# A fused cross-attention and snake MLP on one core: slot tables per block, six batches transposed by DMA, and the squares split between two engines

## The chip, the cores and the metric

One Trainium2 chip, one of its cores. The metric is the device time of one execution, in microseconds (us), and where several runs are shown, their median. Engines: PE (TensorE, matmuls), DVE (VectorE), ACT (ScalarE), POOL (GpSimd) and SP (SyncE, which here only issues DMAs). Each engine takes its instructions strictly in the order of the program; an instruction that waits holds up all behind it on its engine.

## The reference

Eight batches of eight heads; each head has 512 tokens `x` and 32 state rows `state`, both of width 64. Tokens attend to state rows and state rows to tokens; the results, 544 rows per batch, go through an MLP with a snake activation.

```python
scores  = scale * x @ state.T;  a  = softmax(scores);   xread = a @ state     # 512 rows
scores2 = scale * state @ x.T;  a2 = softmax(scores2);  sread = a2 @ x        # 32 rows
y = concat([xread, sread])                     # per head; heads side by side: 4352 x 512
h = y @ w_in                                   # 512 -> 2048
g = h + sin(alpha * h)**2 / (alpha + 1e-9)     # snake
out = g @ w_out                                # 2048 -> 512
```

## The kernel before

The work is a sequence of nine blocks `t`. Blocks 0 to 7 are the 512 token rows of one batch each; block 8 holds the 256 state rows of all batches. A block has 16 slots, one for each 128 columns `f` of the hidden width. Slot `f` of block `t` runs, in the order of the code:

- `mm1(t, f)`: two matmuls into one of four PSUM buffers `h_ps`, then ACT's sine into `s`, then the square `s2 = s * s` on POOL. The token side never forms `xread`: `m_step` multiplies the state rows into `w_in` beforehand (the tile `M`, four steps per batch, cast from PSUM by ACT and DVE), and `mm1` multiplies `M` by the transposed softmax weights `AT`.
- the PE steps that the dictionary `pe` holds for this slot: pieces of the attention of batch `n = t + 1`, and `m_step`.
- `snake`, with a lag of two slots: DVE forms `h + s2 / alpha` from `s2` and `h_ps` into `gT`, which frees the `h_ps` buffer. So `mm1` of slot `f + 4` waits for `snake` of slot `f`.
- the second matmuls `mm2` of the block before (four per slot from block 2 on); when 16 are done ACT copies the sum to `o_sb`, and SP stores it.
- the steps that the dictionary `post` holds.

The attention of a batch consists of `pack` (DVE copies the loaded tile `xnat` to `xp`), `T` (eight PE transposes for each half `g`, and a DVE copy from PSUM to `xT`), `S` (scores), `X` (ACT's exponential `E`, which needs another function table than the sine), `Rs` (row sums and reciprocals on DVE), `N` (normalised weights `A`, on POOL), `AT_` (eight PE transposes and one DVE copy to `AT`), `W` and `Cs` (the state side, with a reciprocal `rC` on DVE). All score, transpose, state and `M` tiles share two PSUM buffers (`tag="px"`).

The order is written out by hand, in `plan(t)`: a tuple of slots for each kind of step, one set for block 0 and one for all others. For block 1 on it reads:

```python
ts, ss, xs, rs, ats = (0, 1), (3, 4), 4, 7, 12
ms = ((9, True, False), (11, True, False), (13, True, False), (15, True, False))
ps = (13, 14)
```

`ts` are the slots of `T`, `ss` of `S`, `xs` of both `X`, `ats` of `AT_`, `ms` of `m_step` with who casts each half (True is ACT), `ps` of `pack` for batch `t + 2`, whose load was issued in slot 5.

Of the kernel before, what the change touches and what calls it, by code (L numbers as in the profile page):

```python
# [10 lines left out]
ALU = mybir.AluOpType  # L11
AX = mybir.AxisListType
BF16 = mybir.dt.bfloat16
FP32 = mybir.dt.float32
U32 = mybir.dt.uint32


@with_exitstack
def kernel(
# [16 lines left out]
    G = 2  # L36
# [13 lines left out]
    apool = ctx.enter_context(tc.tile_pool(name="apool", bufs=2))  # L50
    epool = ctx.enter_context(tc.tile_pool(name="epool", bufs=3))
    smallp = ctx.enter_context(tc.tile_pool(name="smallp", bufs=2))
# [58 lines left out]
    xs_all = const.tile([P, Q, B * Ns], BF16, name="xs_all")  # L111

    def warm_up(n):
        wp = psH.tile([P, S], FP32, name="h_ps")
        for _ in range(n):
            nc.tensor.matmul(wp[:], warm[:, 0:P], warm[:], start=True, stop=True)


    def prep_state():
# [23 lines left out]
    class Att:  # L143
# [2 lines left out]
            a.xp = xppool.tile([P, C, H, D], BF16, name="xp")  # L146

        def alloc(a):
            a.xT = apool.tile([P, Q, S], BF16, name="xT")
# [17 lines left out]
        def T(a, g):  # L167
            tp = psX.tile([P, 2, S], BF16, name="x_ps", tag="px")
            for k in range(2):
                for i in range(C):  # L170
                    nc.tensor.transpose(  # L171
                        tp[:, k, i * P:(i + 1) * P], a.pair(i, 2 * g + k), ident[:]
                    )
            nc.vector.tensor_copy(a.xT[:, 2 * g:2 * g + 2, :], tp[:])  # L174

        def S(a, g):
            sp = psX.tile([P, C, P], FP32, name="s_ps", tag="px")
            for i in range(C):
                for k in range(2):
                    cols = slice(k * 2 * Ns, (k + 1) * 2 * Ns)  # L180
                    nc.tensor.matmul(  # L181
                        sp[:, i, cols],
                        a.xT[:, 2 * g + k, i * P:(i + 1) * P],
                        stT[:, a.b * G + g, cols],
                        start=True, stop=True,
                    )
            a.sp[g] = sp
# [185 lines left out]
    a.AT_([1])  # L373

    def plan(t):
        pe, post = {}, {}

        def add(d, s, fn, *args):  # L380
            d.setdefault(s, []).append((fn, args))

        def nxt(b, k):
            if k == 0:
                atts[b] = Att(b)
            atts[b].pack(k)

        def att(b, m, *args):
            getattr(atts[b], m)(*args)

        n = t + 1
        if t == 0:
            for k in range(2):
                add(post, 0, nxt, 1, k)
            add(pe, 5, m_step, 0, 2, (True, False))
            add(pe, 7, m_step, 0, 3, (True, False))
            ts, ss, xs, rs, ats = (1, 2), (3, 4), 4, 8, 13
            ms, ws = ((9, True, True), (11, True, False), (14, True, False), (15, True, False)), []
            ps = (15, 15)
        else:  # L400
            ts, ss, xs, rs, ats = (0, 1), (3, 4), 4, 7, 12
            ms = ((9, True, False), (11, True, False), (13, True, False), (15, True, False))
            ws = [(6, 7, t)] if n < B else [(0, 1, t)][:B - t]
            if t == 1:
                ws.append((10, 10, 0))
            ps = (13, 14)
        if n < B:
            add(pe, ts[0], att, n, "alloc")
            for g in range(G):
                add(pe, ts[g], att, n, "T", g)  # L410
                add(pe, ss[g], att, n, "S", g)
                add(post, xs, att, n, "X", g)
                add(post, rs + g, att, n, "Rs", g)
                add(post, rs + 1 + g, att, n, "N", g, nc.gpsimd)
            add(pe, ats, att, n, "AT_", [0, 1])
            for k, (s, *on) in enumerate(ms):
                add(pe, s, m_step, n, k, on)
        for s0, s1, b in ws:
            add(pe, s0, att, b, "W")
            add(pe, s1, att, b, "Cs")  # L420
        if t + 2 < B:
            add(post, 5, load_x, t + 2, 1)
            for k in range(2):
                add(post, ps[k], nxt, t + 2, k)

        two = {}
        if t == 0:
            for f in range(9, FT):  # L430
                two[f] = [(0, st, 2 * (f - 9), 2 * (f - 8)) for st in range(2)]
        elif t == 1:
            two[1] = [(0, 0, 14, 16), (0, 1, 14, 16)]
            for f in range(2, FT):
                k0, k1 = 32 * (f - 2) // 14, 32 * (f - 1) // 14
                for h in range(2):
                    a0, a1 = max(k0, 16 * h), min(k1, 16 * h + 16)
                    if a0 < a1:
                        two.setdefault(f, []).append((0, 2 + h, a0 - 16 * h, a1 - 16 * h))
# [55 lines left out]
```

## Time and profile before

| | |
|---|---|
| median of 3 runs | 261.21 us (260.61 to 261.88) |
| the profiled execution, its own time | 260.04 us |
| its span, first to last instruction | 258.3 us |
| mean granted clock of PE | 0.973 |
| busy: PE, DVE, ACT, POOL | 231.3, 169.7, 158.9, 171.4 us |
| blocks 3, 4 and 5, from first `mm1` to first `mm1` | 26.32 us each |

The profiled execution's own time is 1.74 us over its span and 1.17 us under the median. A block's length is read from the time at which the first `mm1` of each block starts: 15.26 (block 0), 43.72, 69.58, 95.90, 122.22, 148.54, 174.86, 201.05 (block 7) and 223.06 us (block 8); the last matmul ends at 251.0 us.

### The profile page before, as it was taken

Reading aid. Unit: us, or ns where it says so; the run is one execution under the profiler, and the core shown is the slowest. Engines: PE = TensorE matmul, PEld = TensorE weight load, DVE = VectorE, ACT = ScalarE, POOL = GpSimd, SP = SyncE. Lnnn points to the kernel's source line nnn. Section 1 sums busy time; section 2 is a strip of 40 time slices with the busy share of each in tenths; the row PEclk is TensorE's granted clock in tenths of the full one; section 3 lists DMA queues with packets and bytes.
Section 4 is the critical chain, followed back from the end, with each engine's and each line's share of the span. In section 5 each row is a group of like instructions: output and inputs, shape, how many; then the busy total and the mean of one; then the engine's idle time right before and its main releaser. Section 6 shows DMA issues by size and latency. Waiting matters only on the chain.

```text
span 258.3 us, 4499 instructions
## 1 busy us (share of the span) xinstructions
PE 231.3 (90%) x1676; PEld 110.7 (43%) x1676; DVE 169.7 (66%) x279; ACT 158.9 (62%) x251; POOL 171.4 (66%) x183
## 2 busy tenths in 40 slices
PE   7575798778999999989998999899999999999980
PEld 2442143333454345434543454345534444555560
DVE  3654857669984897498849884988497765533300
ACT  2668854694759565956595659565966566544410
POOL 8744884649864986498649864996397678744400
PEclk9979599999999999999999999999999999999997
DMA  7999930208011811181118111711111111211111
GB/s 82 195 205 205 203 49 4 82 1 124 0 43 41 122 43 41 41 123 43 43 41 120 46 42 41 121 44 41 44 41 43 41 41 41 83 41 41 44 54 68
DMA packets 19793, 17.85 MB, mean 69 GB/s; under 512 B 2876, under 2 KB 15420, under 8 KB 19772
## 3 DMA queue, kind: packets, MB, share of 16 engines
q0 software_dynamic: 12704, 8.65, 23.6%
q1 hardware_dynamic: 6936, 8.79, 10.2%
q8 instruction: 13, 0.21, 0.3%
q10 hardware_dynamic: 132, 0.13, 0.1%
q14 instruction: 8, 0.07, 0.1%
HBM read 17.31 MB, written 8.91 MB: 102 GB/s over the span
## 4 chain that ended last, share of the span: by engine, by line
PE 69%; DVE 19%; DMA 4%; issue 2%; POOL 2%; ACT 2%; ACTq 0%; POOLq 0%
PE o_ps L314 36%; PE h_ps L288 18%; DVE gT L305 7%; DMA xnat<-in_x_dram 4%; PE m_ps L269 3%; DVE rC L244 3%; PE h_ps L294 3%; DVE R L194 3%; PE x_ps L171 3%; DVE M L280 2%; DVE xs_all L247 2%; PE w_ps L226 1%; PE o_ps L339 1%; PE a_ps L217 1%; DVE rR L195 1%
## 5 line engine op out<-in xcount | busy, mean ns | idle before, releaser
L301 POOL TENSOR_TENSOR s<-s 128x512 bf16<-128x512 bf16 (+1 forms) x144 | 141.5, 992 | 70.5 <-ACT s L299 70.3
L314 PE MATMUL o_ps<-w_out_sb,gT 128*128 128x512 bf16 x528 | 137.3, 382 | 2.6 <-DVE gT L305 2.6
L299 ACT ACTIVATE s<-h_ps,alpha_sb 128x512 bf16<-128x512 f32 (+1 forms) x144 | 94.3, 664 | 72.3 <-PE h_ps L288 61.1
L305 DVE SCALAR_TENSOR_TENSOR gT<-s,inva_sb,h_ps 128x512 bf16<-128x512 bf16 (+1 forms) x144 | 100.1, 711 | 32.0 <-POOL s L301 31.7
L288 PE MATMUL h_ps<-AT,M 128*128 128x512 bf16 x256 | 78.5, 389 | 7.6 <-DVE gT L305 7.1
L314 PEld LDWEIGHTS <-gT 128*128 128x128 bf16 x528 | 46.7, 98 | 52.5 <-issue 6.9
L288 PEld LDWEIGHTS <-M 128*128 128x128 bf16 x256 | 24.9, 99 | 40.5 <-issue 14.3
L280 DVE CAST M<-m_ps 128x512 bf16<-128x512 f32 x29 | 19.6, 676 | 11.5 <-PE m_ps L269 11.4
L320 ACT COPY o_sb<-o_ps 128x512 f32<-128x512 f32 x33 | 19.3, 588 | 9.2 <-PE o_ps L314 7.8
L278 ACT CAST M<-m_ps 128x512 bf16<-128x512 f32 x31 | 17.8, 578 | 0.6 <-PE m_ps L269 0.6
L244 DVE RECIPROCAL rC<-w_ps 128x128 f32<-128x128 f32 x8 | 7.7, 957 | 15.3 <-PE w_ps L237 15.3
L269 PE MATMUL m_ps<-w_in_sb,stT 64*32 64x512 bf16 x240 | 13.5, 401 | 2.8 <-ACT E L190 2.1
L174 DVE COPY xT<-x_ps 128x1024 bf16<-128x1024 bf16 x16 | 11.0, 690 | 5.1 <-PE x_ps L171 4.7
L269 PEld LDWEIGHTS <-stT 64*32 64x32 bf16 x256 | 3.9, 90 | 19.3 <-issue 17.9
L159 DVE COPY xp<-xnat 128x1024 bf16<-128x1024 bf16 x16 | 10.2, 649 | 2.6 <-DMA xnat<-in_x_dram 2.5
L171 PE MATMUL x_ps<-ident,xp 128*128 128x128 bf16 x128 | 10.3, 226 | 1.5 <-ACT stT L140 1.4
L171 PEld LDWEIGHTS <-xp 128*128 128x128 bf16 x128 | 8.9, 102 | 6.0 <-issue 1.7
L194 DVE TENSOR_REDUCE R<-E 128x16 f32<-128x512 bf16 x16 | 10.9, 680 | 0.2 <-ACT E L190 0.2
L190 ACT ACTIVATE E<-s_ps 128x512 bf16<-128x512 f32 x16 | 8.8, 595 | 1.4 <-PE s_ps L181 1.3
L294 PE MATMUL h_ps<-xs_all,w_in_sb 128*128 128x256 bf16 x64 | 9.6, 273 | 0.0
L190 ACT ACT_TABLE_LOAD x7 | 9.0, 1283 | 0.1
L299 ACT ACT_TABLE_LOAD x7 | 9.0, 1283 | 0.1
(46 smaller groups left out, 116.5 us busy)
## 6 DMA issues: line engine op xcount, KB each, us to landing
out_dram<-o_sb SPq DMA_DIRECT2D x33, 256.0 KB, 2.2
xnat<-in_x_dram POOLq DMA_DIRECT2D x7, 512.0 KB, 7.7
w_in_sb<-in_moe_w_in_dram POOLq DMA_DIRECT2D x4, 512.0 KB, 11.0
w_out_sb<-in_moe_w_out_dram POOLq DMA_DIRECT2D x4, 512.0 KB, 19.3
xnat<-in_x_dram POOLq DMA_DIRECT2D x2, 256.0 KB, 5.6
st_nat<-in_state_dram POOLq DMA_DIRECT2D x1, 256.0 KB, 4.5
out_dram<-o_sb SPq DMA_DIRECT2D x1, 128.0 KB
out_dram<-o_sb ACTq DMA_DIRECT2D x1, 128.0 KB
```

Of the source, the lines that this page charges most:

```text
L171: nc.tensor.transpose(tp[:, k, i * P:(i + 1) * P], a.pair(i, 2 * g + k), ident[:])
L190: nc.scalar.activation(a.E[:, g], a.sp[g][:], ACT.Exp, scale=scale)
L194: nc.vector.reduce_sum(a.R[:, g], E8, axis=AX.X)
L269: nc.tensor.matmul(mp[g][o0:o0 + Ns, :], stT[rows, b * G + g, c0:c0 + Ns], w_in_sb[rows, 2 * g + h, fs * FW:(fs + 1) * FW], start=True, st ...
L278: nc.scalar.copy(dst, mp[g][:])
L280: nc.vector.tensor_copy(dst, mp[g][:])
L288: nc.tensor.matmul(hp[:, :n], Ms[t][:, g, f * P:(f + 1) * P], atts[t].AT[:, g, :], start=(g == 0), stop=(g == G - 1),)
L299: nc.scalar.activation(s[:, :n], hp[:, :n], ACT.Sin, scale=alpha_sb[:, f:f + 1])
L301: nc.gpsimd.tensor_tensor(s2[:, :n], s[:, :n], s[:, :n], ALU.mult)
L305: nc.vector.scalar_tensor_tensor(gT[t][:, f, :n], s2[:, :n], inva_sb[:, f:f + 1], hp[:, :n], ALU.mult, ALU.add)
L314: nc.tensor.matmul(op[:], gT[t][:, ft, st * P:(st + 1) * P], w_out_sb[:, ft, :], start=(ft == 0), stop=(ft == FT - 1),)
L320: nc.scalar.copy(o_sb[:], op[:])
```

## The change

- **Tables.** `plan(t)` takes its slots from a table `PLAN` with one entry each for blocks 0, 1, 2 to 6, 7 and 8. The two `X` of a batch may stand in different slots (1 and 5 in blocks 2 to 6), the two `N` may run on different engines (`Nd` lists the halves that DVE takes), and the casts of `M` are given step by step (`MA`). The number of `mm2` per slot is a table too (`two`, `TWO0`, `TWO1`).
- **Transposes by DMA.** For batches 2 to 7 one DMA issued by SP, `T_dma`, transposes the whole `xp` into `xT` (512 KB), a block ahead of its use; another, `AT_dma`, transposes `A` into `AT` (256 KB). The PE transposes and the DVE copies of these batches are gone. Batches 0 and 1 keep them.
- **Squares.** The squares of the slots in `sq` are made by DVE, one slot later and behind that slot's `snake`; 58 of the 144, 35 of them in blocks 2 to 6 (seven each).
- **Buffers.** `xT`, `A`, `AT`, `M` and the small tiles have three buffers in place of two.
- **Ends.** Five more warm-up matmuls stand between the first two `m_step` of block 0; the last store is issued by SP and not by ACT.

```diff
+ 2: {'S': (1, 3), 'X': (1, 5), 'R': (2, 5), 'N': (5, 5), 'A': 5, 'W': (1, 1),
...
+        def T_dma(a):
+            nc.sync.dma_start_transpose(
+                a.xT[:].rearrange("p i q t -> p (i q) t"),
+                a.xp[:].rearrange("p i h d -> p (i h d)"),
+            )
+
+        def AT_dma(a):
+            nc.sync.dma_start_transpose(
+                a.AT[:].rearrange("p g (i t) -> p (g i) t", i=C),
+                a.A[:].rearrange("p g i c -> p (g i c)"),
+            )
...
-        nc.gpsimd.tensor_tensor(s2[:, :n], s[:, :n], s[:, :n], ALU.mult)
+        if f in PLAN[kind(t)]["sq"]:
+            late.append((s2, s, n))
+        else:
+            nc.gpsimd.tensor_tensor(s2[:, :n], s[:, :n], s[:, :n], ALU.mult)
...
+    def squares():
+        while late:
+            s2, s, n = late.pop(0)
+            nc.vector.tensor_tensor(s2[:, :n], s[:, :n], s[:, :n], ALU.mult)
...
-    warm_up(12)
+    warm_up(WARM[0])
...
-    for k in range(2):
-        m_step(0, k, (True, True))
+    m_step(0, 0, (True, True))
+    warm_up(WARM[1])
+    m_step(0, 1, (True, True))
...
+            if t == 0:
+                add(pe, p["A"], att, n, "AT_", [0, 1])
+            else:
+                add(post, p["A"], att, n, "AT_dma")
...
+            add(post, p["L"], load_x, t + 2, 1)
+            add(post, p["P2"][0], first, t + 2)
             for k in range(2):
-                add(post, ps[k], nxt, t + 2, k)
+                add(post, p["P2"][k], att, t + 2, "pack", k)
+            add(post, p["T2"], att, t + 2, "T_dma")
```

In blocks 2 to 6 the table puts `S` in slots 1 and 3, `W` and `Cs` in slot 1, `m_step` in 7, 9, 12 and 14, `pack` in 8 and 10, `T_dma` in 11 and `AT_dma` in 5. In block 0 `T_dma` stands in slot 13 (`pack` in 12), and `S` of that batch in slot 0 of block 1. In block 1 `AT_dma` stands in slot 13, and its `AT` is read by the first `mm1` of block 2.

SP's whole queue, before: one small load, and then the stores.

```order
L68 DMA alpha_sb<-in_moe_alpha_dram 128x16x1
L326 DMA out_dram<-o_sb 128x512 x32
L330 DMA out_dram<-o_sb 4x32x512
L330 DMA out_dram<-o_sb 4x32x256
L490 UNCONDITIONAL_BRANCH
```

SP's queue of the changed kernel, from its start to the stores of block 4.

```order
L122 DMA alpha_sb<-in_moe_alpha_dram 128x16x1
L238 DMA_TRANSPOSE xT<-xp 128x16x128
L408 DMA out_dram<-o_sb 128x512 x3
L238 DMA_TRANSPOSE xT<-xp 128x16x128
L244 DMA_TRANSPOSE AT<-A 128x8x128
L408 DMA out_dram<-o_sb 128x512 x2
L244 DMA_TRANSPOSE AT<-A 128x8x128
L408 DMA out_dram<-o_sb 128x512 x2
L238 DMA_TRANSPOSE xT<-xp 128x16x128
L408 DMA out_dram<-o_sb 128x512 x2
L244 DMA_TRANSPOSE AT<-A 128x8x128
```

Blocks 2 to 5 each have two transposes among their four stores; each transpose waits on SP for the engine that made its input (DVE's `pack`, POOL's `N`).

ACT in the first half of a block in the middle, before: both exponentials of a batch (`E`) stand together between two table loads.

```order
L299 ACTIVATE s<-h_ps,alpha_sb 128x512
L190 ACT_TABLE_LOAD
L190 ACTIVATE E<-s_ps 128x512 x2
L299 ACT_TABLE_LOAD
L299 ACTIVATE s<-h_ps,alpha_sb 128x512 x3
L320 COPY o_sb<-o_ps 128x512
```

The same place in block 3 of the changed kernel.

```order
L263 ACT_TABLE_LOAD
L263 ACTIVATE E<-s_ps 128x512
L372 ACT_TABLE_LOAD
L372 ACTIVATE s<-h_ps,alpha_sb 128x512 x2
L402 COPY o_sb<-o_ps 128x512
L372 ACTIVATE s<-h_ps,alpha_sb 128x512 x2
L263 ACT_TABLE_LOAD
L263 ACTIVATE E<-s_ps 128x512
L372 ACT_TABLE_LOAD
L372 ACTIVATE s<-h_ps,alpha_sb 128x512
L402 COPY o_sb<-o_ps 128x512
```

The exponentials are apart, with two table loads each: four loads in a block where there were two (24 against 14 over all blocks).

DVE at the end of one block and the beginning of the next, before.

```order
L159 COPY xp<-xnat 128x4x256
L280 CAST M<-m_ps 128x512
L305 SCALAR_TENSOR_TENSOR gT<-s_1209,inva_sb,h_ps 128x512
L174 COPY xT<-x_ps 128x1024
L305 SCALAR_TENSOR_TENSOR gT<-s_1235,inva_sb,h_ps 128x512
L174 COPY xT<-x_ps 128x1024
L305 SCALAR_TENSOR_TENSOR gT<-s_1248,inva_sb,h_ps 128x512
```

DVE in the last slots of block 3 and the first of block 4 of the changed kernel; `s_...<-s` is a square.

```order
L217 COPY xp<-xnat 128x4x256
L387 SCALAR_TENSOR_TENSOR gT<-s_1438,inva_sb,h_ps 128x512
L353 CAST M<-m_ps 128x512
L387 SCALAR_TENSOR_TENSOR gT<-s_1459,inva_sb,h_ps 128x512
L384 TENSOR_TENSOR s_1476<-s 128x512
L384 TENSOR_TENSOR s_1487<-s 128x512
L387 SCALAR_TENSOR_TENSOR gT<-s_1476,inva_sb,h_ps 128x512
L387 SCALAR_TENSOR_TENSOR gT<-s_1487,inva_sb,h_ps 128x512
L387 SCALAR_TENSOR_TENSOR gT<-s_1510,inva_sb,h_ps 128x512
L384 TENSOR_TENSOR s_1521<-s 128x512
L384 TENSOR_TENSOR s_1543<-s 128x512
L387 SCALAR_TENSOR_TENSOR gT<-s_1521,inva_sb,h_ps 128x512
```

The two copies of `xT` are gone, and squares stand in pairs ahead of the snakes that read them.

## Rows read from the trace of the kernel before

**Rows 1.** The page's first part: busy us, share of the span and instructions of each engine.

```profile
PE 231.3 (90%) x1676; PEld 110.7 (43%) x1676; DVE 169.7 (66%) x279; ACT 158.9 (62%) x251; POOL 171.4 (66%) x183
```

**Rows 2.** Busy time of each engine in blocks 0, 1 and 3.

```profile
core 0: us, PE busy (x) PEld busy (x) DVE busy (x) ACT busy (x) POOL busy (x), PEclk, DMA share, GB/s
15.26:43.72 28.46, 22.76 (x149) 8.94 (x149) 18.11 (x31) 18.27 (x28) 19.54 (x19) 0.82 0.84 134
43.72:69.58 25.86, 21.65 (x189) 10.07 (x188) 19.72 (x34) 17.44 (x27) 18.16 (x19) 1.00 0.28 52
...
95.90:122.22 26.32, 25.64 (x193) 11.96 (x192) 20.22 (x33) 18.18 (x29) 19.21 (x20) 1.00 0.29 61
```

**Rows 3.** Waits inside block 3: who waited for whom, us, times, longest.

```profile
ACT s L299 <- PE h_ps L288: 7.6, 9, 1.2
...
PE h_ps L288 <- DVE gT L305: 0.7, 2, 0.5
```

**Rows 4.** PE's timeline around block 3: start, us, instruction; the first `mm1` of six slots.

```profile
89.38 0.59 PE L288 MATMUL h_ps<-AT,M 128*128 128x512 bf16 x2
...
91.12 0.59 PE L288 MATMUL h_ps<-AT,M 128*128 128x512 bf16 x2
...
92.86 0.60 PE L288 MATMUL h_ps<-AT,M 128*128 128x512 bf16 x2
...
97.64 0.60 PE L288 MATMUL h_ps<-AT,M 128*128 128x512 bf16 x2
...
99.38 0.60 PE L288 MATMUL h_ps<-AT,M 128*128 128x512 bf16 x2
...
100.68 0.60 PE L288 MATMUL h_ps<-AT,M 128*128 128x512 bf16 x2
```

**Rows 5.** Groups in block 3: busy us, mean ns of one.

```profile
L280 DVE CAST M<-m_ps 128x512 bf16<-128x512 f32 x5 | 3.4, 673 | 0.8 <-PE m_ps L269 0.8
L278 ACT CAST M<-m_ps 128x512 bf16<-128x512 f32 x5 | 2.9, 577 | 0.0
...
L174 DVE COPY xT<-x_ps 128x1024 bf16<-128x1024 bf16 x2 | 1.4, 692 | 0.5 <-PE x_ps L171 0.4
...
L190 ACT ACT_TABLE_LOAD x1 | 1.3, 1283 | 0.0
...
L220 DVE COPY AT<-a_ps 128x1024 bf16<-128x1024 bf16 x1 | 0.7, 691 | 0.4 <-PE a_ps L217 0.4
```

**Rows 6.** Timeline of POOL and DVE, at 12 us and at 94 us.

```profile
12.49 1.06 POOL L202 TENSOR_TENSOR A<-E,rR 128x512 bf16<-128x512 bf16 x1
...
13.26 0.85 DVE L205 TENSOR_TENSOR A<-E,rR 128x512 bf16<-128x512 bf16 x1
...
94.32 1.04 POOL L301 TENSOR_TENSOR s<-s 128x512 bf16<-128x512 bf16 x1 [0.62 <-ACT s L299]
...
94.57 1.07 DVE L159 COPY xp<-xnat 128x1024 bf16<-128x1024 bf16 x1
```

**Rows 7.** All copies of `xp`: shortest, median and longest ns.

```profile
L159 DVE COPY xp<-xnat x16: 411/572/1073, 7.1 to 173.5; 128x1024 bf16<-128x1024 bf16 x16
```

**Rows 8.** The page's DMA parts: SP's queue (packets, MB, share), and issues to landing.

```profile
q1 hardware_dynamic: 6936, 8.79, 10.2%
...
out_dram<-o_sb SPq DMA_DIRECT2D x33, 256.0 KB, 2.2
xnat<-in_x_dram POOLq DMA_DIRECT2D x7, 512.0 KB, 7.7
```

**Rows 9.** Bytes moved in 40 slices of 100 to 112 us, a lone store in it.

```profile
GB/s 0 0 0 0 0 0 0 0 0 0 0 0 48 396 369 62 0 0 0 0 0 0 0 0 0 0 0 0 0 0 0 0 0 0 20 341 239 205 118 123
```

**Rows 10.** Bytes moved in 40 slices of the first 50 us.

```profile
GB/s 0 3 41 177 182 152 191 203 206 209 197 199 202 205 207 212 201 208 207 206 204 207 207 206 199 194 186 29 0 0 0 13 0 0 7 0 0 7 0 200
```

**Rows 11.** DVE's longest wait in blocks 0 and 1 (15.26 to 69.58 us).

```profile
DVE M L280 <- PE m_ps L269: 6.5, 5, 3.0
```

More of the change, by code (lines that the diff above doesn't have):

```diff
@@ L15 @@
 U32 = mybir.dt.uint32
+PLAN = {0: {'P': (0, 0),
+     'T': (1, 1),
+     'S': (2, 2),
+     'X': (3, 3),
+     'R': (3, 8),
+     'N': (9, 10),
+     'A': 15,
+     'M0': (5, 8),
+     'M': (9, 11, 12, 14),
+     'MA': ((1, 0), (1, 1), (1, 1), (1, 1)),
+     'L': 1,
+     'P2': (12, 12),
+     'T2': 13,
+     'sq': (0, 9, 10, 12, 13),
+     'Nd': ()},
+ 1: {'S': (0, 2),
+     'X': (2, 2),
+     'R': (4, 7),
+     'N': (4, 7),
+     'A': 13,
+     'W': (4, 5),
+     'W0': (10, 11),
+     'M': (7, 8, 12, 14),
+     'MA': ((1, 0), (1, 1), (1, 1), (1, 1)),
+     'L': 2,
+     'P2': (9, 10),
+     'T2': 10,
+     'sq': (1, 8, 14),
+     'Nd': (0,)},
+ 2: {'S': (1, 3),
+     'X': (1, 5),
+     'R': (2, 5),
+     'N': (5, 5),
+     'A': 5,
+     'W': (1, 1),
+     'M': (7, 9, 12, 14),
+     'MA': ((1, 0), (1, 1), (0, 1), (1, 1)),
+     'L': 4,
+     'P2': (8, 10),
+     'T2': 11,
+     'sq': (0, 4, 5, 11, 12, 14, 15),
+     'Nd': (0,),
+     'two': (4, 6, 4, 6, 5, 6, 5, 4, 5, 1, 4, 3, 2, 3, 3, 3)},
+ 7: {'W': (3, 5), 'sq': (0, 3, 4, 6, 8, 13, 14, 15), 'Nd': (1,)},
+ 8: {'sq': (3, 4, 8, 9, 11, 13, 14), 'Nd': (0,)}}
+TWO0 = (0, 0, 0, 0, 0, 4, 0, 0, 2, 2, 4, 4, 4, 0, 2, 4)
+TWO1 = (0, 1, 8, 0, 2, 2, 7, 3, 6, 4, 0, 3, 1, 0, 1, 0)
+WARM = (12, 5, 0)
 @with_exitstack
@@ L49 @@
     xppool = ctx.enter_context(tc.tile_pool(name="xppool", bufs=4))
-    apool = ctx.enter_context(tc.tile_pool(name="apool", bufs=2))
+    apool = ctx.enter_context(tc.tile_pool(name="apool", bufs=3))
     epool = ctx.enter_context(tc.tile_pool(name="epool", bufs=3))
-    smallp = ctx.enter_context(tc.tile_pool(name="smallp", bufs=2))
+    smallp = ctx.enter_context(tc.tile_pool(name="smallp", bufs=3))
     gpool = ctx.enter_context(tc.tile_pool(name="gpool", bufs=2))
@@ L113, in warm_up, with kind @@
     def warm_up(n):
-        wp = psH.tile([P, S], FP32, name="h_ps")
+        if n:
+            wp = psO.tile([P, S], FP32, name="o_ps")
         for _ in range(n):
             nc.tensor.matmul(wp[:], warm[:, 0:P], warm[:], start=True, stop=True)
+    def kind(t):
+        return t if t < 2 or t >= B - 1 else 2
     def prep_state():
@@ L148, in alloc @@
         def alloc(a):
-            a.xT = apool.tile([P, Q, S], BF16, name="xT")
+            a.xT = apool.tile([P, C, Q, P], BF16, name="xT")
             a.E = epool.tile([P, G, C, P], BF16, name="E")
@@ L173, in T @@
                     )
-            nc.vector.tensor_copy(a.xT[:, 2 * g:2 * g + 2, :], tp[:])
+            nc.vector.tensor_copy(
+                a.xT[:, :, 2 * g:2 * g + 2, :],
+                tp[:].rearrange("p k (i t) -> p i k t", i=C),
+            )
[8 more added lines that the diff above has]
+                a.A[:].rearrange("p g i c -> p (g i c)"),
+            )
         def S(a, g):
@@ L182, in S @@
                         sp[:, i, cols],
-                        a.xT[:, 2 * g + k, i * P:(i + 1) * P],
+                        a.xT[:, i, 2 * g + k, :],
                         stT[:, a.b * G + g, cols],
@@ L347, in mm2_last @@
                 nc.vector.tensor_copy(o_sb[:, cols], op[:, cols])
-                store(t, st, o_sb, cols, nc.scalar)
-    atts, Ms, gT, ops = {}, {}, {}, {}
-    warm_up(12)
+                store(t, st, o_sb, cols, nc.sync)
+    atts, Ms, gT, ops, late = {}, {}, {}, {}, []
+    warm_up(WARM[0])
     prep_state()
@@ L369, with first @@
     a.N(1, nc.vector)
-    for k in range(2):
-        m_step(0, k, (True, True))
+    m_step(0, 0, (True, True))
+    warm_up(WARM[1])
+    m_step(0, 1, (True, True))
     a.AT_([0])
     a.AT_([1])
+    warm_up(WARM[2])
     def plan(t):
         pe, post = {}, {}
+        p = PLAN[kind(t)]
         def add(d, s, fn, *args):
             d.setdefault(s, []).append((fn, args))
[L383 to L386, printed above, removed]
+        def first(b):
+            atts[b] = Att(b)
+            atts[b].alloc()
         def att(b, m, *args):
@@ L392, in plan @@
         if t == 0:
-            for k in range(2):
[L394 to L420, printed above, removed]
@@ L421, in plan @@
-        if t + 2 < B:
-            add(post, 5, load_x, t + 2, 1)
-            for k in range(2):
-                add(post, ps[k], nxt, t + 2, k)
+            add(post, p["P"][0], first, 1)
+            for g in range(G):
+                add(post, p["P"][g], att, 1, "pack", g)
+                add(pe, p["T"][g], att, 1, "T", g)
+                add(pe, p["M0"][g], m_step, 0, 2 + g, (True, False))
+        if n < B:
+            for g in range(G):
+                add(pe, p["S"][g], att, n, "S", g)
+                add(post, p["X"][g], att, n, "X", g)
+                add(post, p["R"][g], att, n, "Rs", g)
+                add(post, p["N"][g], att, n, "N", g, nc.vector if g in p["Nd"] else nc.gpsimd)
+            if t == 0:
+                add(pe, p["A"], att, n, "AT_", [0, 1])
+            else:
+                add(post, p["A"], att, n, "AT_dma")
+            for k, s in enumerate(p["M"]):
+                add(pe, s, m_step, n, k, p["MA"][k])
@@ L428, in plan @@
+        for key, b in (("W", t), ("W0", 0)):
+            if key in p:
+                add(pe, p[key][0], att, b, "W")
+                add(pe, p[key][1], att, b, "Cs")
+        if t + 2 < B:
+            add(post, p["L"], load_x, t + 2, 1)
+            add(post, p["P2"][0], first, t + 2)
+            for k in range(2):
+                add(post, p["P2"][k], att, t + 2, "pack", k)
+            add(post, p["T2"], att, t + 2, "T_dma")
         two = {}
         if t == 0:
-            for f in range(9, FT):
-                two[f] = [(0, st, 2 * (f - 9), 2 * (f - 8)) for st in range(2)]
-        elif t == 1:
[L433 to L439, printed above, removed]
-        else:
-            for f in range(FT):
-                two[f] = [(t - 1, f // 4, (f % 4) * 4, (f % 4) * 4 + 4)]
+            k = 0
+            for f, c in enumerate(TWO0):
+                if c:
+                    two[f] = [(0, st, k, k + c // 2) for st in range(2)]
+                    k += c // 2
+        elif t == 1:
+            k0 = sum(TWO0) // 2
+            todo = [(st, ft) for ft in range(k0, FT) for st in (0, 1)]
+            todo += [(st, ft) for st in (2, 3) for ft in range(FT)]
+            for f, c in enumerate(TWO1):
+                two[f] = [(0, st, ft, ft + 1) for st, ft in todo[:c]]
+                todo = todo[c:]
+            assert not todo
+        else:
+            todo = [(st, ft) for st in range(C) for ft in range(FT)]
+            for f, c in enumerate(p.get("two", (4,) * FT)):
+                two[f] = [(t - 1, st, ft, ft + 1) for st, ft in todo[:c]]
+                todo = todo[c:]
+            assert not todo
@@ L450 @@
         for f in range(FT):
+            due = len(late)
             cur = mm1(t, f)
@@ L456 @@
                 snake(*pend.pop(0))
+            if due:
+                squares()
             for args in two.get(f, []):
@@ L460 @@
                 fn(*args)
+    squares()
     while pend:
```

## The prediction

> **What bounds the kernel now.** I read the page's busy shares first: PE 90%, no other engine over 66% [rows 1]. A share over the whole span hides the stages, so next the busy time block by block [rows 2]. In block 3, as in 2, 4 and 5, PE is busy 25.64 of 26.32 us, DVE 20.22, POOL 19.21, ACT 18.18. The waits of that block say the same: ACT waits 7.6 us for PE, while PE waits only 0.7 us in all, for the `snake` that frees an `h_ps` buffer [rows 3]. So blocks 2 to 6 are bound by PE, and what leaves PE's queue there shortens the block, until another engine comes to its limit. Blocks 0 and 1 are different: 28.46 and 25.86 us with no engine over 22.8 busy [rows 2], and DVE standing 6.5 us behind `m_ps` tiles that are late [rows 11]. They lose time to the order. Blocks 7 and 8 have PE busy throughout and nothing here leaves their queue, so I leave them at their time.
>
> **PE's transposes.** The price is read from the starts of slots. A plain slot, two `mm1` and four `mm2`, takes 100.68 - 99.38 = 1.30 us, so 0.216 us for a matmul of 512 columns; a slot with eight `T` takes 99.38 - 97.64 = 1.74, one with eight `AT_` takes 91.12 - 89.38 = 1.74, one with an `m_step` takes 92.86 - 91.12 = 1.74 [rows 4]. Each group of eight transposes thus costs PE 0.44 us. A block from 1 to 6 loses three such groups, 1.32 us. Blocks 2 to 6 come down to 26.32 - 1.32 = 25.0, and to 25.0 - 0.7 = 24.3 if the tables also remove PE's waits.
>
> **What the other engines then hold in blocks 2 to 6.** DVE: 20.22, less two `xT` copies (1.38), the `AT` copy (0.69) and two casts (2 x 0.673) [rows 5], is 16.8. It gains seven squares and one `N`. The trace has no square on DVE. Below, it costs no less than the shortest `xp` copy, 0.41 us [rows 7]; above, the one `N` that DVE ran, 0.85 [rows 6]. That `N` started at 13.26 while POOL's ended at 13.55; without those 0.29 us it is 0.56. It is the nearest row (two SBUF inputs, 512 elements), so I take 0.55: 16.8 + 8 x 0.55 = 21.2, with bounds 20.1 and 23.6. ACT: 18.18 + two more table loads (2.57) + two more casts (1.15) [rows 5] = 21.9. POOL: 19.21 - 8 x 1.04 = 10.9. All are under 24.3, but DVE and ACT are now within 10 to 13% of PE, in queues that can't be reordered. I walked the order of block 3 by these durations: the tightest places are `snake` 10 to 12, behind an `xp` copy, a cast and two squares, where `mm1` 14 and 15 would find their buffer free with about 0.1 us to spare. Some waits of PE will stay, so I take a block of 24.8 (24.3 to 25.6): -1.5 each, -7.6 for five.
>
> The trace does show that DVE and POOL hinder each other: an `xp` copy that started at 94.57 took 1.07 us, ending 0.28 after POOL's square of 94.32 to 95.36, where the shortest took 0.41 [rows 6, 7]. The Trainium skill (SBUF — State Buffer, Who interferes with whom) has the rule: a DVE instruction with two SBUF inputs and a GpSimd instruction that reads SBUF exclude each other for a whole instruction. By that rule every square on DVE may wait for one on POOL; what it would make of the time is the second rival.
>
> **The transposes by DMA.** None is in the trace. For `xT` (512 KB) the lower bound is a store: 256 KB land 2.2 us after the issue [rows 8], and a lone store moves at up to 396 GB/s [rows 9], 0.66 us for 256 KB; so 2.2 + 0.66 = 2.9. The upper bound counts pieces: SP's queue spends 0.102 x 16 x 258.3 / 6936 = 61 ns on a packet [rows 8]; `xp` is read in 2048 rows of 128 elements, 256 bytes each, so 2048 x 61 ns / 16 = 7.8, and 1.5 of latency (2.2 - 0.66): 9.3 us. The loads of `xnat`, 7.7 us [rows 8], lie between, but those read twice the bytes. I take 5 us, nearer to the store, which goes by the same queue. For `AT`, half as large: 2.2 to 5.4, taken 3.3.
>
> The Trainium skill (DMA: Bandwidth & Descriptors, Latency and other measured facts) states 261 GB/s for such a transpose with a non-contiguous middle dimension, and about 2 us fixed for a DMA. By that `xT` would land in some 4 us, an estimate, and the sum below would be about 1 us lower.
>
> Where are they waited for? In blocks 2 to 6, from `T_dma` in slot 11 to `S` in slot 1, PE has 15 `mm2` (3.2), six `mm1` pairs (2.6) and two `m_step` (0.9): 6.7 us of cover over 5. `AT_dma` in slot 5 has ten slots. Neither costs anything while that cover holds. A waiting transpose also holds SP's stores behind it, but `o_sb` has three buffers and four stores per block, so a store two slots late delays no one. Two places have less cover. In block 0 `T_dma` follows the `pack` of batch 2, whose load is the last of a stream that fills the DMA engines until 27 slices of 1.25 us, 33.7 us [rows 10]; with two copies of 0.43 and 5 us, `S` can't start before 39.6 us. In block 1 `AT_dma` stands in slot 13 and its `AT` opens block 2: behind it PE has five matmuls and an `m_step`, 1.5 to 1.8 us, against 3.3. That is a stall of 1.5 us.
>
> **Blocks 0 and 1.** Block 0 runs from 15.26 to 43.72. Its exponentials and its late `m_step` are drawn apart, which is aimed at the 6.5 us of [rows 11]; DVE there holds 18.1 less two casts plus five squares, 19.5, from 16.6 on. A walk of DVE's queue ends at about 38.4, but the transposed `xT` is there at 39.6 or later. I let block 1 start at 40.3: -3.5 (-5.5 if all fits and the DMA takes 2.9). Block 1 holds ACT 19.8 (17.44 + three casts and a store copy), PE 20.8 (21.65 - 1.32 + two more `mm2`) [rows 2, 5], DVE about 18.5. I take 22.5 for its 25.86: -3.4 (-2 to -4.5). The five warm-up matmuls fill a wait for `w_in` and cost nothing. The last store by SP, which is idle by then, -0.6 to 0: -0.3.
>
> **The sum.** -7.6 - 3.5 - 3.4 + 1.5 - 0.3 = -13.3 against the profiled 260.04: 246.7 in that execution, and with the 1.17 by which the median lay above it, 248.
>
> **Rivals.**
> 1. *The transposes land late.* The mechanism is PE standing at `S` in each block from 2 to 6, and SP's stores behind it. With L for the landing of `xT`, the cost over my sum is (L - 5) at block 0, half of that at block 2, and 5 x (L - 6.7) once L is over 6.7. At L = 8 it is 4.5 + 6.5 = 11 and the time 259; at 9.3, 6.5 + 13 = 19.5 and 267. It turns the sign at about L = 8.4. For it speaks the packet price, against it the store. L over 6.7 but under 8.4: 0.12, about 256. L over 8.4, the case on the other side: 0.11, 262 to 267.
> 2. *DVE becomes the bound through POOL.* If each of the seven squares, the `N` and the two copies waits as the three of [rows 6, 7] did (0.64, 0.29 and, for the median copy, 0.16; mean 0.36), DVE holds 21.2 + 8 x 0.36 = 24.1, and with its wait for `W` and `Cs` at the beginning of a block about 25.4. The blocks give 0.9 each, 4.6, and half of the gain of blocks 0 and 1 is lost: 260.04 - 4.6 - 3.5 + 1.5 - 0.3 + 1.17 = 254. Chance 0.17. For it: two of three copies and `N` met POOL busy. Against: POOL falls from 19.2 to 10.9 us, so it is met less often.
> 3. *ACT's two table loads more.* Each switch stops the sines for 2 x 1.28 + 0.59. If a stop uses up the four `h_ps` buffers, PE waits up to 0.6 us twice in a block: 25.5, a time of 252. Chance 0.08.
> 4. *The gain is not there:* PE's waits grow by what leaves its queue, in all blocks, and the order of blocks 0 and 1 gives nothing either; 259 to 262. Chance 0.06.
>
> **How the numbers follow.** My forecast has 0.46, its own range 242 to 252: the lower end with squares at 0.41, blocks of 24.3 and `xT` in 2.9, the upper with blocks of 25.6. With rivals 1 to 3 the range must reach to 262; I give 241 to 262, which leaves out the worst of rival 1. Half a per cent, 1.3 us, is about what this measurement can tell from no change. Faster: 0.46 + 0.12 + 0.17 + 0.08 = 0.83, less 0.02 for late landings near the turn, 0.81; slower: 0.11 and half of rival 4, 0.14; same: 0.05.
>
> **What would show it.** Right: blocks 2 to 6 start 24.3 to 25.2 us apart with PE busy over 24; no wait of PE's `s_ps` for a DMA from block 2 on; a wait for `AT`'s DMA of 1 to 2 us at the start of block 2; squares on DVE of 0.4 to 0.7 us. Wrong: `DMA_TRANSPOSE` to landing over 6.7 us and PE waiting for it in each block (rival 1); DVE busy over 23 per block with squares near 0.9 (rival 2); PE's `mm1` waiting for `snake` right after each second table load (rival 3).

## The result, and the profile after

The changed kernel takes 242.54 us (median of 4 runs, 241.71 to 242.94) against 260.91 for the kernel before on the same chip: a ratio of 0.929, interval 0.925 to 0.9325. Run again later, unchanged (`e12`), it gave 241.93 (ratio 0.927, 0.9246 to 0.9295). It is faster, inside the range, and the gain of 18 us is larger than the 13 of the forecast. One execution each of `e5` and `e10` ran more than 1.5% longer than the fastest of its kernel and is left out of the times given below.

The page of the changed kernel: busy shares, some groups, and the DMA issues.

```profile
PE 221.1 (92%) x1537; PEld 103.4 (43%) x1537; DVE 170.4 (71%) x310; ACT 176.4 (74%) x276; POOL 110.4 (46%) x119
...
L384 DVE TENSOR_TENSOR s<-s 128x512 bf16<-128x512 bf16 (+1 forms) x58 | 23.0, 405 | 7.5 <-ACT s L372 7.1
...
L263 ACT ACT_TABLE_LOAD x12 | 15.4, 1283 | 0.2
...
xT<-xp SPq DMA_TRANSPOSE x6, 4.5
AT<-A SPq DMA_TRANSPOSE x6, 3.1
```

PE lost 10 us of busy time [rows 1] while the span fell by 18.4 (258.3 to 239.9): the other 8 were waits. The 10 are not all transposes: 3.6 of them are in block 0 (22.76 to 19.15), where the mean granted clock was 0.82 before [rows 2] and is 1.00 now. Windows of the changed kernel for blocks 0 to 3, cut where the first `mm1` of a block starts (columns as in [rows 2]):

```profile
16.13:39.41 23.28, 19.15 (x146) 7.92 (x146) 17.98 (x34) 18.42 (x30) 13.38 (x14) 1.00 1.10 165
39.41:63.46 24.05, 20.74 (x168) 8.62 (x166) 19.22 (x33) 18.33 (x29) 14.96 (x15) 1.00 0.55 104
63.46:87.37 23.91, 23.91 (x169) 10.79 (x170) 19.67 (x36) 21.74 (x34) 12.55 (x12) 1.00 0.48 99
87.37:111.26 23.89, 23.89 (x169) 10.76 (x168) 19.53 (x36) 21.30 (x33) 11.50 (x11) 1.00 0.50 100
```

In block 3 PE is busy for every microsecond of 23.89, where it stood for 0.68 of 26.32 [rows 2]. ACT is up to 21.30 and POOL down to 11.50. From the first `mm1` of block 2 (63.46) to that of block 7 (182.95) are 119.49 us, against 131.47 before: -12.0. Up to the start of block 2 the gain is 69.58 - 63.46 = 6.1, behind the start of block 8 it is 0.3, in block 7, 22.0 us in both, nothing.

PE's waits of the changed kernel in blocks 0 and 1 show where the transposes are still waited for.

```profile
PE h_ps L361 <- DVE gT L387: 1.3, 3, 0.7
PE s_ps L254 <- DMA xT<-xp: 1.3, 1, 1.3
...
PE h_ps L361 <- DMA AT<-A: 0.5, 1, 0.5
```

The wait for `xT` is batch 2's, at the start of block 1; the wait for `AT` is for the same batch, at the start of block 2. From 87.37 to 182.95 us the same view has no row for PE at all.

### The profile page after: what moved, and what is told of

It reads as the page before. It is cut to its first block, busy times and chain, and to the rows that moved or that the text cites. A ratio compares the mean times of both kernels' runs of the same rounds, so it can differ in the third digit from the quotient of the medians.

```text
span 239.9 us, 4210 instructions
## 1 busy us (share of the span) xinstructions
PE 221.1 (92%) x1537; PEld 103.4 (43%) x1537; DVE 170.4 (71%) x310; ACT 176.4 (74%) x276; POOL 110.4 (46%) x119
## 4 chain that ended last, share of the span: by engine, by line
PE 75%; DMA 14%; issue 3%; POOL 2%; DVE 2%; ACT 1%; POOLq 0%
PE o_ps L396 44%; PE h_ps L361 19%; DMA xnat<-in_x_dram 7%; DMA w_in_sb<-in_moe_w_in_dram 3%; PE m_ps L342 3%; PE h_ps L367 3%; DMA xT<-xp 2%; DMA AT<-A 2%; PE o_ps L421 1%; PE w_ps L299 1%; ACT s L372 1%; PE s_ps L254 1%; PE w_ps L310 1%; POOL s L377 1%; PE o_ps L171 1%
## 5 line engine op out<-in xcount | busy, mean ns | idle before, releaser
L396 PE MATMUL o_ps<-w_out_sb,gT 128*128 128x512 bf16 x528 | 135.9, 380 | 1.4 <-DMA w_out_sb<-in_moe_w_out_dram 1.0
L377 POOL TENSOR_TENSOR s<-s 128x512 bf16<-128x512 bf16 (+1 forms) x86 | 86.2, 1016 | 93.0 <-ACT s L372 80.9
L372 ACT ACTIVATE s<-h_ps,alpha_sb 128x512 bf16<-128x512 f32 (+1 forms) x144 | 95.0, 674 | 39.7 <-PE h_ps L361 25.8
L361 PE MATMUL h_ps<-AT,M 128*128 128x512 bf16 x256 | 75.6, 379 | 2.4 <-DVE gT L387 1.5
L396 PEld LDWEIGHTS <-gT 128*128 128x128 bf16 x528 | 48.6, 98 | 57.8 <-issue 8.5
L361 PEld LDWEIGHTS <-M 128*128 128x128 bf16 x256 | 24.7, 98 | 32.5 <-issue 4.6
L384 DVE TENSOR_TENSOR s<-s 128x512 bf16<-128x512 bf16 (+1 forms) x58 | 23.0, 405 | 7.5 <-ACT s L372 7.1
L351 ACT CAST M<-m_ps 128x512 bf16<-128x512 f32 x46 | 25.5, 599 | 0.2 <-PE m_ps L342 0.2
L267 DVE TENSOR_REDUCE R<-E 128x16 f32<-128x512 bf16 x16 | 10.9, 680 | 8.0 <-ACT E L263 8.0
L278 POOL TENSOR_TENSOR A<-E,rR 128x512 bf16<-128x512 bf16 x7 | 7.3, 1043 | 19.6 <-issue 12.0
L353 DVE CAST M<-m_ps 128x512 bf16<-128x512 f32 x14 | 9.6, 684 | 2.4 <-PE m_ps L342 2.2
L217 DVE COPY xp<-xnat 128x1024 bf16<-128x1024 bf16 x16 | 8.2, 525 | 3.5 <-DMA xnat<-in_x_dram 3.5
L171 PE MATMUL o_ps<-warm 128*128 128x512 bf16 x17 | 7.1, 597 | 1.3 <-DVE warm L157 1.3
```

Of the source, the lines that this page charges most:

```text
L267: nc.vector.reduce_sum(a.R[:, g], E8, axis=AX.X)
L351: nc.scalar.copy(dst, mp[g][:])
L361: nc.tensor.matmul(hp[:, :n], Ms[t][:, g, f * P:(f + 1) * P], atts[t].AT[:, g, :], start=(g == 0), stop=(g == G - 1),)
L384: nc.vector.tensor_tensor(s2[:, :n], s[:, :n], s[:, :n], ALU.mult)
L396: nc.tensor.matmul(op[:], gT[t][:, ft, st * P:(st + 1) * P], w_out_sb[:, ft, :], start=(ft == 0), stop=(ft == FT - 1),)
```

## The experiments

Each ratio is to the kernel before, run on the same chip; block lengths are read as above, or, where a trace lacks matmul records, from ACT's sines.

**PE's transposes back, tables kept** (`e1`). `T` stands in slot 11 of the block before its use (13 in blocks 0 and 1), `AT_` in slot 8.

```diff
-                add(post, p["A"], att, n, "AT_dma")
+            add(pe, {0: 15, 1: 9}.get(t, 8), att, n, "AT_", [0, 1])
-            add(post, p["T2"], att, t + 2, "T_dma")
+            for g in range(G):
+                add(pe, {0: 13, 1: 13}.get(t, 11), att, t + 2, "T", g)
```

> The changed kernel with the transposes of batches 2 to 7 back on PE (T in slot 11 of the block before, 13 in blocks 0 and 1; AT_ in slot 8, in block 1 in slot 9), tables and squares kept. Theory A (PE's queue is the block, each transposing group costs its 0.44 us): blocks 2 to 5 of 23.9 + 1.32 = 25.2 us, block 6 of 24.3, the two waits for a transposing DMA gone; 242.5 + 4 x 1.32 + 0.44 + 1.3 (block 1) - 1.7 = about 248. Rival (the order alone brings the gain, the transposes were covered anyway): 242 to 244. A third (DVE gets 2.1 us of copies per block and becomes the bound with them): blocks over 26, 252 or more.

251.3 us, 0.964 (0.961 to 0.966). Blocks 2 to 5 take 25.28, 1.38 over the changed kernel, close to the three groups of 0.44 (1.32) that were read from [rows 4]. PE is busy throughout; the window of block 3:

```profile
92.02:117.30 25.28, 25.28 (x194) 12.11 (x192) 21.20 (x39) 21.42 (x33) 11.40 (x11) 1.00 0.28 63
```

Block 0 takes 27.12, 3.8 more; that was not in the sum, and is why the total came out above what was expected. Of it 0.9 are batch 2's two groups of `T`, which run at 36.57 without a wait for the load; the granted clock in block 0 is 0.94 here and 1.00 in the changed kernel. How the rest divides is open.

**Transposes by DMA alone, in the order of before** (`e2`): `T_dma` after `pack`, `AT_dma` in the place of `AT_`, three buffers.

```diff
+            if k == 1 and b > 1:
+                atts[b].T_dma()
...
-                add(pe, ts[g], att, n, "T", g)
+                if n == 1:
+                    add(pe, ts[g], att, n, "T", g)
```

> The kernel before with nothing changed but the transposes of batches 2 to 7, made by DMA (issued behind the second pack and behind N). Theory A (PE's own waits, 26.32 - 25.34 = 1.0 us per block by the starts of its slots, need the new order or the shared squares to go): blocks 2 to 5 of 25.0 us, 260.9 - 6 x 1.32 = about 253. Rival (POOL's squares, 19.2 us per block and late behind the table loads, become the bound once PE is shorter): blocks of 25.5 to 26.3, 256 to 260. Rival (the transposes bring nearly all): under 250.

253.63, 0.9725 (0.9705 to 0.975). Blocks 3 to 5 start 24.98 apart: 26.32 - 1.32 = 25.0 to the digit. So 7.0 us are the transposes', and the other 11 to 12 come from the rest of the change. By the traces 5.7 of these are in blocks 2 to 6 and 6.2 ahead of them: block 2 starts at 69.71 here, with a granted clock of 0.79 in block 0, and at 63.46 in the changed kernel. Both waits of PE for `snake` stay, at slots 9 and 11 of the block, as large as before [rows 3]; in block 3:

```profile
PE h_ps L303 <- DVE gT L320: 0.7, 2, 0.5
```

**All squares and `N` on POOL, tables kept** (`e3`): every `sq` and `Nd` empty.

> The changed kernel with all squares and both N of each batch on POOL, tables and DMA transposes kept. Theory A (sharing the squares removes PE's waits for the snake): POOL at 19.2 of 23.9 us, behind each of the two table switches it starts 3 us late and can't catch up, PE waits return: blocks of 24.5 to 25.3, blocks 0 and 1 longer by 2 to 4 us together, 247 to 252. Rival (the squares need not move, the tables do it): 242 to 243.5.

244.12, 0.937 (0.934 to 0.939). I had expected the blocks to be longer, and was wrong: blocks 2 to 6 take 23.90, no worse, although POOL is busy for some 19.4 of them; 24 us in blocks 2 and 3:

```profile
86.00:110.00 24.00, 24.00 (x170) 10.75 (x168) 16.68 (x28) 21.35 (x33) 19.45 (x20) 1.00 0.49 99
```

Only the beginning is longer: block 2 starts at 66.7, not 63.5. The squares and `N` on DVE buy about 2 us. Of the 3.3 in the trace 2.3 are block 1's (26.38 against 24.05, both at a granted clock of 1.00); the rest, in block 0, is no more than kernels with the same block 0 differ by (`e7`). In the trace the two copies of batch 2's `pack` take 1.27 and 1.26 us beside POOL's squares, against 0.43 and 0.42 in the changed kernel, so `T_dma` starts later (37.7, not 36.0) and PE waits 2.4 us for `xT`, not 1.3.

**Both exponentials together** (`e4`), which saves two table loads a block.

```diff
-     'X': (1, 5),
-     'R': (2, 5),
+     'X': (3, 3),
+     'R': (4, 5),
```

> The changed kernel with both exponentials of a batch in slot 3 in blocks 2 to 6, so two table loads per block in place of four. Theory A (PE is the bound and the second switch is hidden): ACT falls from 21.3 to 18.7 us per block, blocks stay at 23.9, 242.0 to 243.0. Rival (the loads take time off PE, or the longer single stop of ACT does): blocks differ from 23.9 by more than 0.3, over 2 us in all, either way.

246.4, 0.946 (0.942 to 0.95): blocks 2 to 6 take 24.87, 0.97 more, though ACT has 2.57 less to do. The timeline of DVE and PE in block 3 of this kernel:

```profile
99.43 0.42 DVE L384 TENSOR_TENSOR s<-s 128x512 bf16<-128x512 bf16 x1 [0.94 <-ACT s L372]
...
102.54 0.59 PE L361 MATMUL h_ps<-AT,M 128*128 128x512 bf16 x2 [0.81 <-DVE gT L387]
```

ACT stops once for 2 x 1.28 + 2 x 0.59 us (loads and exponentials), and DVE stands 0.94 us for the first sine behind the stop. Then DVE has two squares, `N`, a row sum and its reciprocal to do before the `snake` (at 101.83) that PE's `mm1` waits for. With two shorter stops, four slots apart, there is no such wait. But with `X` the row sum moved too, from slot 2 to 4; how much of the 0.97 is the longer stop and how much what stands behind it on DVE was not tested apart. The two table loads more, which I had held for a risk (rival 3), come with a wait less.

**`T_dma` later** (`e5`): slot 15 in place of 11 in blocks 2 to 5.

```diff
-     'T2': 11,
+     'T2': 15,
```

> The changed kernel with T_dma of blocks 2 to 5 in slot 15 in place of 11, nothing else. Theory A (the landing of 4.5 us is hidden only by the PE work between issue and S): from slot 15 to S in slot 1 PE has 1.7 us, and the issue comes behind the store of slot 15 on SP, about 1 us later than the slot's end; S waits 3 to 4 us for the DMA at the start of blocks 3 to 6, these blocks' starts shift by 12 to 16 us in all, 254 to 258. Rival (the transposes land faster when issued beside less traffic, or PE's wait is absorbed by the h_ps buffers later): 243 to 247.

266.07, 1.02 (1.015 to 1.025): slower than before, by some 2%. The waits and the windows of this kernel:

```profile
PE s_ps L254 <- DMA xT<-xp: 16.0, 5, 3.8
```

```profile
93.00:122.00 29.00, 24.70 (x165) 11.51 (x168) 19.54 (x35) 21.50 (x32) 11.54 (x11) 0.95 0.41 83
122.00:152.00 30.00, 25.28 (x169) 11.28 (x173) 19.71 (x35) 21.50 (x32) 11.52 (x11) 0.92 0.38 79
152.00:182.00 30.00, 25.90 (x165) 11.62 (x165) 19.70 (x35) 21.50 (x32) 11.52 (x11) 0.90 0.39 79
```

PE waits up to 3.8 us for each `xT`. Four of the five waits, 15.1 us, are in blocks 3 to 6, but these blocks are longer by 24.1 together: the granted clock, 1.00 in the same blocks of the changed kernel, is 0.95, then 0.92 and 0.90. The cover counted for `T_dma` in slot 11 is needed, and rival 1's mechanism is real and dearer than I had it.

**Squares in other slots** (`e6`): as many on DVE, but alternating with POOL's.

```diff
-     'sq': (0, 4, 5, 11, 12, 14, 15),
+     'sq': (1, 3, 6, 8, 10, 12, 14),
```

> The changed kernel with DVE's seven squares of blocks 2 to 6 in alternate slots (1, 3, 6, 8, 10, 12, 14), so that they run beside POOL's squares, where in the changed kernel nearly all stood where POOL was idle. Theory lock (a DVE square that finds POOL at work waits for the end of its instruction): mean of the DVE squares from 0.42 to 0.6 to 0.9 us, longest over 1.2, DVE over 20.5 us per block; with PE the bound, blocks of 23.9 to 24.3, 242.5 to 245. Rival (no exclusion for a product of a tile with itself): squares stay at 0.42, blocks at 23.9, 242.5.

246.83, 0.946 (0.943 to 0.949); blocks of 24.81, 0.9 more. All squares of DVE (min/median/max ns) in this kernel, then in the changed one:

```profile
L384 DVE TENSOR_TENSOR s<-s x58: 291/418/1258, 19.2 to 229.9; 128x512 bf16<-128x512 bf16 x51, 128x256 bf16<-128x256 bf16 x7
```

```profile
L384 DVE TENSOR_TENSOR s<-s x58: 293/418/426, 19.4 to 224.4; 128x512 bf16<-128x512 bf16 x51, 128x256 bf16<-128x256 bf16 x7
```

And the timeline of POOL and DVE in this kernel, in one block:

```profile
106.24 1.04 POOL L377 TENSOR_TENSOR s<-s 128x512 bf16<-128x512 bf16 x1 [0.60 <-ACT s L372]
...
106.50 1.07 DVE L384 TENSOR_TENSOR s<-s 128x512 bf16<-128x512 bf16 x1
```

Fifteen of the 51 full squares ran into one on POOL, and each ended 0.28 us after POOL's (107.57 against 107.28 here). In the changed kernel none did; one ran into the end of an `N` on POOL and took 0.42 all the same. From start to start PE's gaps in this block are 0.22 ahead of `mm1` 12 and 0.71 ahead of `mm1` 14, and each of the two `snake` that end them stands behind a square that met POOL's (0.65 and 0.51 us lost). But the squares also stand in other places of DVE's queue, the second ahead of a cast and that `snake`; how much of the 0.9 is the meeting, and how much the place, is not parted.

**Block 1 with more cover** (`e7`): `S` from slots (0, 2) to (2, 3), `X` from 2 to 3, `AT_dma` from 13 to 9.

> The changed kernel with, in block 1 alone, S in slots 2 and 3 (were 0 and 2), both X in slot 3, AT_dma in slot 9 (was 13). Theory A (block 1 loses PE's two waits for a transposing DMA, 1.3 and 0.5 us, and has slack elsewhere): both waits gone, block 1 from 24.05 to 22.3 to 23.2, 241.0 to 241.8. Rival (block 1 is held by the snake chain, the waits only stand where it would have waited anyway): 242.2 to 243.

242.08, 0.927 (0.924 to 0.931): no different from the changed kernel. Both waits for a DMA are gone, but PE then waits 2.1 us in one piece for ACT's exponential (`w_ps`). Block 1 takes 23.5, 0.2 to 0.6 less than in the two traces of the changed kernel. The end of block 0 lies between 39.2 and 40.8 us in kernels with the same block 0, which hides anything as small. It goes with the granted clock of block 0: 39.2 to 39.7 where that is 1.00 (the changed kernel twice, `e4`), 40.0 and 40.7 at 0.93 (`e5`, `e6`), 40.8 at 0.87 (here).

**Batch 2 later still** (`e11`): `pack` and `T_dma` in slot 15 of block 0, `S` in slots 4 and 5, and the rest of block 1 behind it.

> The changed kernel with batch 2 a little later: in block 0 its pack and its T_dma in slot 15 (were 12 and 13), in block 1 S in 4 and 5, X in 5, row sums and N in 7 and 8, W in 2 and 3, m_step in 8, 9, 12, 14, AT_dma in 9. Theory A (block 0 ends late because DVE, in order, stands at the pack until the last load has landed, and block 1 begins with a wait for the transpose): both gone, blocks 0 and 1 shorter by 1.5 to 3 us together, 239.5 to 241. Rival (blocks 0 and 1 are held elsewhere, and the later attention of batch 2 makes block 1 longer): 242 to 244.

244.26, 0.935 (0.932 to 0.938), some 2 us worse. DVE no longer stands behind the late load in block 0 (0.6 us in the changed kernel), but block 2 starts at 65.7: in block 1 PE now waits 1.8 us for `snake`, 1.1 for `xs_all` and 0.7 for a cast of `M`, where the changed kernel has 1.3 for `xT`, 0.5 for `AT` and 0.7 for `E`.

**Fewer warm-ups** (`e8`): `WARM = (12, 0, 0)`.

> The changed kernel without the five warm-up matmuls between the first two m_step. Theory A (they keep PE's granted clock up through block 0 and cost nothing, since they fill a wait for w_in): without them the clock falls behind that wait, block 0 takes 1 to 2 us longer, 243.5 to 244.5. Rival (PE is not the bound in block 0, so its clock there is worth nothing): 242.0 to 243.0.

242.28, 0.929 (0.927 to 0.932), against 241.93 for the changed kernel on the same chip; the times overlap, so what the five warm-up matmuls are worth, if anything, is not clear of noise. The clock did move as theory A has it: the mean of an execution is 0.974 to 0.982 without them and 0.984 to 0.992 with them (four each). In the trace it is 0.84 in block 0, which takes 25.40 us, against 1.00 and 23.28 in the changed kernel; but `e7`, with the warm-ups in place, has 0.87 and 25.64, so one trace of each doesn't settle it.

**Exponentials apart in the old order** (`e9`): `e2` with `S` in slots 2 and 4 and `X` in 2 and 6.

> The kernel before with the transposes of batches 2 to 7 by DMA and, in blocks 1 to 7, S in slots 2 and 4 and X in slots 2 and 6 in place of both in slot 4; squares on POOL, all other slots as before. Theory A (the 1.0 us per block that PE waited came from ACT's stop of two exponentials between two table loads): blocks 2 to 6 of 23.9 to 24.1, 248.5 to 249.5. Rival (it came from the hand-made order as a whole, casts and packs among the snakes): blocks of 24.6 to 25.0, 252 to 254.

259.63, 0.996 (0.994 to 0.999). A miss: the waits at slots 9 and 11 remain (from start to start 0.36 and 0.50, in `e2` 0.36 and 0.63), and since `S` stands earlier while `T_dma` stays in slot 14, PE waits 1.1 us a block for `xT`. The second is a fault of the experiment; the first says that parting the exponentials is not enough by itself.

**Steps spread in the old order** (`e10`): `e2` with `W` and `Cs` in slot 1, `Rs` in slots 7 and 10 and each `N` one slot later, `AT_dma` in slot 11.

> The kernel before with the transposes of batches 2 to 7 by DMA and, in blocks 1 to 7, W and Cs in slot 1 (were 6 and 7) and the second row sum with its reciprocal in slot 10 (was 8), so that DVE's extra work no longer stands in one heap between slots 7 and 9 behind ACT's stop; both X stay together in slot 4, squares on POOL. Theory heap (in the order of before PE waited at slots 9 and 11 because DVE's rC, xs and both R stood among the snakes just when ACT had stopped): blocks 2 to 6 of 23.9 to 24.3 in place of 24.98, 249.0 to 250.5. Theory stop (the joined stop of ACT costs the 1.0 us by itself, as joining it did in the new order): blocks of 24.8 to 25.0, 253 to 254.

268.12, 1.03 (1.024 to 1.036), slower than before, with blocks of 27.8 that neither theory had. The timeline of this kernel at the end of block 2:

```profile
93.96 4.02 POOL L316 TENSOR_TENSOR s<-s 128x512 bf16<-128x512 bf16 x4
...
94.47 3.80 DVE L159 COPY xp<-xnat 128x1024 bf16<-128x1024 bf16 x1
...
98.19 0.73 DVE L320 SCALAR_TENSOR_TENSOR gT<-s,inva_sb,h_ps 128x512 bf16<-128x512 bf16 x1
...
98.98 0.38 PE L303 MATMUL h_ps<-AT,M 128*128 128x512 bf16 x1 [1.86 <-DVE gT L320]
```

The later `N` leaves POOL four squares behind, which it then runs in a row. (The kernel before has such a row too, but the first copy of `xp` meets only its last 0.3 us.) DVE's copy of `xp`, 0.41 us at its shortest, starts in the first of the four and ends 0.29 us after the last, 3.80 us later; the `snake` behind it is late, and PE stands for 1.86 us. Blocks 3 to 5 repeat it (3.80 us each time). This is rival 2's lock in full, from a place where I had not looked for it. Neither theory is settled by it: ahead of slots 9 to 11 of block 3 PE's gaps are 1.01, 0.21 and nothing, where `e2` has 0.36, nothing and 0.63.

## Why the prediction was nearly right

The mechanism was right: the kernel was bound by PE in blocks 2 to 6, the transposes leave its queue, the DMAs are hidden there, and no other engine becomes the bound. The size was off in one term, and the agreement in blocks 0 and 1 is in part luck.

- **Blocks 2 to 6, the mis-sized term: -7.6 forecast, -12.0 measured.** "24.8 (24.3 to 25.6)" is 23.9; even the lower bound was too high. The transposes' 1.32 stand (`e2`: 24.98; `e1`: 1.38). The step that failed is "25.0 - 0.7 = 24.3 if the tables also remove PE's waits", and "some waits of PE will stay" behind it. The timeline of the kernel before shows both waits of block 3:

```profile
110.30 0.59 PE L288 MATMUL h_ps<-AT,M 128*128 128x512 bf16 x2 [0.21 <-DVE gT L305]
...
113.97 0.59 PE L288 MATMUL h_ps<-AT,M 128*128 128x512 bf16 x2 [0.47 <-DVE gT L305]
```

These make the 0.7. But the matmul ahead of each is drawn 0.38 us long, while the next one can start 0.216 after it. From start to start the gaps are 0.59 and 0.85 where 0.22 is due: 0.37 + 0.63 = 1.0. With it, 26.32 - 1.32 - 1.0 = 24.0, 0.1 over the measured block. I had priced the matmuls by starts and the waits by a view that counts from modelled ends. None of the waits stayed, and the allowance of 0.5 a block for them is the larger part of the error.
- **What removed the waits** is the table's order: the transposes alone leave them (`e2`), and without a square on DVE they are gone as well (`e3`). Parting the exponentials, with the row sums that follow them, is needed in this order (`e4`, +0.97), but parting doesn't do it alone in the old one (`e9`). Which of the other moves has to go with it stays open: `e9` is blurred by its late `T_dma`, `e10` by the stop behind POOL.
- **DVE's squares.** "I take 0.55": 0.42, next to the lower bound. The 0.56 came from an `N`, which is no measure for a square: on DVE it takes 0.68 here. The two `xp` copies of a block also fell, from 1.64 to 1.17. So DVE holds 19.5 a block, not 21.2. ACT, 21.3 (21.9), and POOL, 11.5 (10.9), came near.
- **The transposes.** `xT` lands in 4.5 us (4.3 to 5.2; 5 taken), `AT` in 3.1 (3.3 taken). The estimate of some 4 us from the Trainium skill (DMA: Bandwidth & Descriptors, Latency and other measured facts) is 0.5 too low here.
- **Blocks 0 and 1, with the stall at block 2:** -5.4 forecast, -6.1 measured. Block 0 takes 23.3 and block 1 starts at 39.4 (40.3); block 1 takes 24.05, against 22.5 + 1.5 in the forecast. That the parts come so near is luck in two places. The stall for `AT` is 0.5, not 1.5, and one of 1.3 for batch 2's `xT` stands in its place: its load is copied from 35.2 on, not 33.7, and `S` runs at 41.27, not 39.6. The sum let this delay the start of block 1, but `S` comes behind the first `mm1` of block 1 and so delays what follows it there. And the sum has no term for the granted clock, which in block 0 went from 0.82 [rows 2] to 1.00: kernels with the new block 0 take 23.3 to 24.7 for it at 1.00 and 25.6 at 0.87 (`e7`). So 0.9 to 2.3 us, an estimate from these traces, may be the clock's; whether the new order raised it is not shown. Nor is it shown that the two waits set the time: `e7` and `e11` remove both, and another wait takes their place. Tail and block 7: as forecast.
- **The rivals.** 1 did not occur: `xT` lands in 4.5 with 6.7 of cover, but 4 slots later it makes the kernel slower than before (`e5`). 2 did not occur in the changed kernel, where no square of DVE runs into one of POOL's; with other slots the meetings come, and a block loses the 0.9 that I gave the rival, though not by the meetings alone as far as is known (`e6`). My reason against it, that POOL is less busy, was not the point: POOL is as idle in `e6`. 3 did not occur; putting the exponentials together costs time (`e4`). 4 did not occur.

The forecast of -13.3, 4.4 more in blocks 2 to 6, and 0.7 more at the beginning make the 18.4 that the span lost.

## What to carry to other kernels

Price a wait as you price the work, from start to start of the waiting engine's instructions, and not from the idle time behind a modelled end: here that turned 0.7 us a block into 1.0. One long stop of an engine for a function switch can cost more than two short ones with two more table loads: here 0.97 us a block, together with what had to move behind the stop. When DVE and POOL share work, look where their instructions meet and what stands behind them: the same division of the squares was worth 0.9 us a block more or less by its slots alone.

## What the runs showed of the hardware

- A copy on DVE that starts while POOL works on SBUF tiles can wait not for one instruction of POOL but for a whole row of them: it took 3.80 us beside four squares (`e10`, four times) and ended 0.29 us after the last; squares of DVE ended 0.28 us after the one they met (`e6`). The Trainium skill (SBUF — State Buffer, Who interferes with whom) gives the lock, which the trace bears out, for one instruction; that the waiting copy doesn't get in between two instructions of POOL is what the run adds.
- When PE stood for 3.7 to 3.8 us once in a block, the mean granted clock of blocks with the same matmuls fell from 1.00 to 0.95, 0.92 and 0.90, so that part of them ran at the lower of its two levels (`e5`): the late transpose made four blocks longer by 24.1 us together, and only 15.1 of them are in the waits.
- Issuing a transpose keeps SP for 1.64 us (`xT`) and 1.24 us (`AT`) by the medians of its instructions, time in which a store behind it isn't issued.
